# The low half of x in a gated linear attention with FFN: a GpSimd subtraction for nine units

## The chip, the cores and the metric

The kernel runs on one core of one Trainium2 chip. The metric is the device time of one execution in microseconds, median of several runs. The core has five engines that matter here: TensorE (PE, with its weight loads as PEld), VectorE (DVE), ScalarE (ACT), GpSimd (POOL) and the queue of SyncE (SPq) that issues the DMAs. Each works through its own list of instructions in order and waits on semaphores for the others.

## The reference

A gated linear attention runs over 4 batches, 8 heads, 768 steps and a head size of 48, all in float32; a feed-forward layer follows on the 3072 tokens:

```python
for t in range(S):
    state = alpha[:, :, t, :, None] * state + np.einsum('bhd,bhe->bhde', k[:, :, t], v[:, :, t])
    y[:, :, t] = np.einsum('bhd,bhde->bhe', q[:, :, t], state)
x = np.ascontiguousarray(y.transpose(0, 2, 1, 3)).reshape(B * S, H * D)
h = x @ w_in
g = np.maximum(0.01 * h, h)
out = (g @ w_out).astype(np.float32)
```

`x` is 3072 x 384, `w_in` 384 x 2048 and `w_out` 2048 x 384. The weights arrive as 64-bit floats.

## The kernel before

**Units and blocks.** The attention is cut into 24 units, each one chunk of 128 steps of one batch (`units`, six chunks by four batches). Three units make a block of 384 tokens, so the feed-forward layer has eight blocks, and it walks through the hidden dimension in 16 slices `f` of 128. The first nine units (`AHEAD`) are worked ahead of the bulk of the feed-forward layer, by `attention` (L518); the other fifteen are woven into it by `attention_later` (L548).

**One unit.** `scans` (L315) brings alpha into channel-by-time form, for the first nine units by four TensorE transposes into a PSUM bank (L287), and runs the running products (`pc`, four VectorE scans) and the reversed scan (`rc`). `scaled_q` and `scaled_k` multiply q and k by them (`qs`, `ks`). `scores` multiplies `ks` by `qs` on TensorE into two banks (16 matmuls, issued at L465). `mask_scores` (L377) copies them to SBUF on ScalarE (`sm`, L384) and zeroes the upper triangle on GpSimd (L385), one instruction for each of two halves; behind the masks GpSimd also runs the pending state scalings (L391). `k_tokens` transposes `ks` back (L398, evicted at L400), and `sum_up` (L344) makes a range check on ScalarE. `past`, `values` and `products` are the matmuls that make the unit's output y in one PSUM bank and the new state; `past` exists from each batch's second chunk on, that is from unit 4. `values` reads the masked scores. `split` (L469) then takes y out of PSUM.

**Low and high halves.** All feed-forward products are made from two halves: a value rounded to the fast matmul format (`fp32r`), called high, and the rest, called low. A slice of the first layer is nine matmuls, three 128-row groups by three pairs (high by high, high weight by low x, low weight by high x), at L597. ScalarE then makes 0.01 h (L602), VectorE the maximum (L605), ScalarE the high half of g (L607), VectorE its low half (L611), and nine matmuls at L626 make the second layer. In `split`, x's high half is a ScalarE copy from PSUM (L476), and its low half a VectorE subtraction, y from PSUM minus the high half from SBUF (L477). VectorE instructions of the attention are issued through the helper `vector` (L276), so the trace has them on that line: the subtraction is the one that writes `large`, the tile that holds x.

**Converting the weights.** `converting` (L248 to L268) turns a slice of 64-bit weights into a high and a low 32-bit half with two ScalarE instructions and six VectorE instructions; five of these read and write SBUF tiles alone. Slices 0, 1 and 2 are converted while units 6, 7 and 8 run; the others run beside the first two blocks of the feed-forward layer (`items` alternates blocks 0 and 1 over f, then takes blocks 2 to 7 one at a time).

**What sets the order.** Within the first nine units the order in each engine's list is not written out: the build puts each instruction where it becomes ready, earlier-traced ones first, on a timeline of its own. `tc.issue_after` (through `behind`) pins single ones: state scalings behind the mask, the first weight loads behind certain loads of v, the first conversions behind `AFTER` and `BEGIN`. One of these keys is `("xh", 6)`, the ScalarE copy of unit 6 in `split`. PSUM tiles of the attention come from two rings of three banks (`a` and `b`); a bank is free again when its last reader is done. `gather` (L507) moves the last rows of x into place by DMA after each third unit.

## Time and profile before

| What | Value |
| --- | --- |
| Median of 3 runs | 524.14 us (523.52 to 524.3) |
| The profiled execution's own time | 523.46 us |
| Its span in the profile | 521.7 us |
| TensorE busy | 507.4 us, 97% of the span |
| VectorE busy | 380.4 us, 73% |
| ScalarE busy | 236.0 us, 45% |
| GpSimd busy | 75.9 us, 15% |
| Granted TensorE clock, mean | 0.997 |
| The nine subtractions in VectorE's list, start | 17.56, 22.37, 27.18, 32.02, 37.79, 44.69, 51.80, 59.34, 65.81 us |

The span is the time from the first to the last instruction in the profile; 1.76 us of the execution's own time lie outside it. Shares are averages over stages with different limits: GpSimd's 15% over the whole span is 4 to 5 tenths in each slice of the first 65 us and nothing from there to 150 us. In the rows of the trace, a time in brackets at the end of a row is idle time of that engine just before the instruction, with what ended it. Matmuls overlap, so a matmul's duration (some 0.27 to 0.34 us) is longer than the step from one to the next.

### The profile page before, as it was taken

To read this page: it belongs to the slowest core of one execution; us is meant where nothing else is said; L and a number is where in the kernel's file an instruction comes from. 1 tells how busy PE (TensorE), PEld (TensorE's weight loads), DVE (VectorE), ACT (ScalarE), POOL (GpSimd) and SP (SyncE) were. 2 spreads that over 40 slices of the span, in tenths; PEclk is the share of its full clock that TensorE was granted. 3 is DMA by queue.
4 is the path that set the end of the run, shared out by engine and by line. 5 is a ranking of instruction groups with operands and counts; after the bars stand their busy time and mean duration, and the time that the engine had idled before them with its cause. 6 is when DMAs were issued, how large, how long until landed. Compare 5 with 4: busy or idle time off the path is not lost.

```text
span 521.7 us, 10758 instructions
## 1 busy us (share of the span) xinstructions
PE 507.4 (97%) x4178; PEld 487.6 (93%) x4178; DVE 380.4 (73%) x710; ACT 236.0 (45%) x504; POOL 75.9 (15%) x143
## 2 busy tenths in 40 slices
PE   8998999999999999999999999999999999999995
PEld 8787899999989889999999999999999999999995
DVE  6999999999999776778587677686586683333331
ACT  1765755555544543444443543453443542334331
POOL 4555500000001201121120120102102000000000
PEclk9999999999999999999999999999999999999998
DMA  9999985445715431542233421523421001001001
GB/s 145 163 186 187 233 178 134 121 123 143 178 32 151 118 72 44 123 97 85 63 76 65 128 69 32 122 57 89 99 57 40 27 21 25 0 1 45 1 0 52
DMA packets 92985, 46.68 MB, mean 89 GB/s; under 512 B 57856, under 2 KB 90112, under 8 KB 92928
## 3 DMA queue, kind: packets, MB, share of 16 engines
q1 hardware_dynamic: 92928, 45.93, 40.5%
q8 instruction: 35, 0.57, 0.5%
q14 instruction: 22, 0.18, 0.1%
HBM read 38.83 MB, written 4.72 MB: 83 GB/s over the span
## 4 chain that ended last, share of the span: by engine, by line
PE 72%; DVE 16%; DMA 5%; issue 3%; SPq 2%; ACT 1%; DVEq 0%; ACTq 0%
PE b L626 29%; PE ph L597 28%; PE a L465 8%; DMA raw<-in_moe_w_in_dram 3%; DVE pw L265 2%; DVE bits L254 2%; DVE bits L263 2%; PE b L465 2%; DVE gl L611 2%; DVE t L605 2%; PE ph L465 1%; DVE bits L251 1%; PE a L398 1%; PE b L287 1%; DVE pw L261 1%
## 5 line engine op out<-in xcount | busy, mean ns | idle before, releaser
L597 PE MATMUL ph<-large,w 128*128 128x384 f32 x1152 | 224.5, 336 | 1.1 <-DVE t L605 0.8
L597 PEld LDWEIGHTS ph<-large,w 128*128 128x128 f32 x1152 | 200.6, 188 | 3.4 <-DVE t L605 1.1
L626 PE MATMUL b<-w,gh 128*128 128x384 f32 x672 | 168.9, 338 | 0.6 <-DVE t L605 0.6
L605 DVE TENSOR_TENSOR t<-ph,t 128x384 f32<-128x384 f32 x128 | 70.6, 552 | 98.5 <-ACT t L602 98.1
L602 ACT ACTIVATE t<-ph 128x384 f32<-128x384 f32 x128 | 62.6, 489 | 136.0 <-PE ph L597 135.6
L626 PEld LDWEIGHTS b<-w,gh 128*128 128x128 f32 x672 | 119.6, 188 | 2.2 <-DVE t L605 0.8
L607 ACT CAST gh<-t 128x384 fp32r<-128x384 f32 x128 | 65.8, 514 | 95.2 <-DVE t L605 95.1
L626 PE MATMUL b<-w,gl 128*128 128x384 f32 x336 | 108.3, 335 | 0.0
L611 DVE TENSOR_TENSOR gl<-t,gh 128x384 fp32r<-128x384 f32 x128 | 70.7, 552 | 18.9 <-ACT gh L607 18.7
L626 PEld LDWEIGHTS b<-w,gl 128*128 128x128 f32 x336 | 62.7, 188 | 0.0
L385 POOL TENSOR_SCALAR_AFFINE_SELECT sm<-sm 128x512 f32<-128x512 f32 x33 | 24.7, 760 | 129.1 <-ACT sm L384 115.4
L335 POOL COPY small<-up 128x4 f32<-128x4 f32 x15 | 4.7, 313 | 199.6 <-DVE up L276 199.6
L465 PE MATMUL a<-qs,ks 48*64 48x128 f32 (+1 forms) x552 | 26.3, 272 | 3.0 <-DVE ks L276 1.5
L465 PEld LDWEIGHTS a<-qs,ks 48*64 48x64 f32 (+1 forms) x552 | 22.4, 140 | 4.7 <-ACT gh L607 1.5
L384 ACT COPY sm<-a 128x512 f32<-128x512 f32 x24 | 14.0, 583 | 14.7 <-PE b L465 12.5
L626 PE MATMUL a<-w,gh 128*128 128x384 f32 x96 | 20.5, 334 | 0.0
L276 DVE TENSOR_TENSOR_SCAN up<-e,small 128x128 f32<-128x128 f32 x60 | 20.4, 402 | 0.0
L276 DVE TENSOR_TENSOR_SCAN down<-e,small 128x511 f32<-128x511 f32 x15 | 19.2, 1282 | 0.7
L391 POOL TENSOR_TENSOR small<-small 48x192 f32<-48x192 f32 x32 | 19.0, 595 | 1.2
L257 ACT CAST w<-bits 128x768 fp32r<-128x768 f32 x16 | 13.4, 838 | 9.2 <-DVE bits L254 8.5
L276 DVE STREAM_TRANSPOSE e<-small 128x512 f32<-128x512 f32 x15 | 17.2, 1144 | 0.0
L626 PEld LDWEIGHTS a<-w,gh 128*128 128x128 f32 x96 | 17.0, 188 | 0.0
(106 smaller groups left out, 578.5 us busy)
## 6 DMA issues: line engine op xcount, KB each, us to landing
raw<-in_moe_w_out_dram SPq DMA_DIRECT2D x16, 384.0 KB, 4.0
small<-in_v_dram SPq DMA_DIRECT2D x24, 192.0 KB, 3.8
raw<-in_moe_w_in_dram SPq DMA_DIRECT2D x32, 144.0 KB, 4.4
out_dram<-o SPq DMA_DIRECT2D x24, 192.0 KB, 1.9
small<-in_alpha_dram SPq DMA_DIRECT2D x32, 96.0 KB, 2.2
small<-in_q_dram SPq DMA_DIRECT2D x30, 96.0 KB, 2.1
small<-in_k_dram SPq DMA_DIRECT2D x30, 96.0 KB, 2.2
small<-in_alpha_dram SPq DMA_DIRECT2D x30, 80.0 KB, 2.3
```

What stands on the lines that cost most here:

```text
L257: made["hi", f] = put(ordered, "ACT", lambda: nc.scalar.copy(hi, val))
L276: return put(u >= AHEAD, "DVE", lambda: op(*args))
L384: made["sm", u] = nc.scalar.copy(sm[s], ss[s])
L385: made["mask", u] = nc.gpsimd.affine_select(out=sm[s], in_=sm[s], compare_op=ALU.is_ge, fill=0.0, base=0, pattern=[[0, NP], [1, C]], chann ...
L391: nc.gpsimd.tensor_tensor(*scalings.pop(0))
L465: made["product",] = nc.tensor.matmul(out, weights, moving, start=start, stop=stop, skip_group_check=True)
L597: product = nc.tensor.matmul(ph, w_in_of(f, wn, g), xt[:, g, :], start=n == 0, stop=n == 3 * NG - 1)
L602: put(ordered, "ACT", lambda: nc.scalar.mul(t, ph, 0.01))
L605: put(ordered, "DVE", lambda: nc.vector.tensor_tensor(t, ph, t, ALU.max))
L607: put(ordered, "ACT", lambda: nc.scalar.copy(gh, t))
L611: made["gl", i, f] = put(ordered, "DVE", lambda: nc.vector.tensor_tensor(gl, t, gh.bitcast(F32), ALU.subtract))
L626: product = nc.tensor.matmul(po[j], gt[:, js], w_out_of(f, wn), start=f == 0 and n == 0, stop=f == NF - 1 and n == 2)
```

## The change

For the first nine units, `split` reads y from PSUM twice on ScalarE: one copy to a new SBUF tile `full` in full float32, one to the high half in `large` as before. The subtraction then runs on GpSimd, `full` minus the high half, both in SBUF. VectorE no longer takes part, and y's PSUM bank is now last read by the second ScalarE copy. `full` is 128 x 512 float32 with two buffers. The key `("xh", u)` now names the first of the two copies. Units 9 to 23 keep their form.

```diff
         xh, xl = (x_sb[0:BR, at:at + NP, n, j * C:(j + 1) * C] for n in (0, 1))
+        if u < AHEAD:
+            full = atp.tile([P, NP, C], F32, name="full")
+            made["xh", u] = nc.scalar.copy(full[0:BR], y[0:BR])
+            nc.scalar.copy(xh, y[0:BR])
+            made["x", u] = nc.gpsimd.tensor_tensor(xl, full[0:BR], xh.bitcast(F32), ALU.subtract)
+            return
         for h, l, t in [(xh, xl, y)] if u < AHEAD else [(xh[:, s::2, :], xl[:, s::2, :], pair[s]) for s in (1, 0)]:
             made["xh", u] = nc.scalar.copy(h, t[0:BR])
             made["x", u] = vector(u, nc.vector.tensor_tensor, l, t[0:BR], h.bitcast(F32), ALU.subtract)
```

## Prediction

> **What bounds the kernel now.** I read the page's head first, then the busy time of each engine by stage, cut at 28, 41 and 65 us, then the waits and the timelines within these stages.

> ```profile
> PE 507.4 (97%) x4178; PEld 487.6 (93%) x4178; DVE 380.4 (73%) x710; ACT 236.0 (45%) x504; POOL 75.9 (15%) x143
> 15.00:28.00 13.00, 12.55 (x167) 10.34 (x163) 12.67 (x28) 9.43 (x24) 7.30 (x18) 1.00 1.10 163
> 28.00:41.00 13.00, 12.83 (x181) 10.71 (x183) 11.38 (x25) 8.61 (x23) 7.62 (x17) 1.00 1.13 193
> 41.00:65.00 24.00, 21.66 (x274) 18.76 (x270) 23.48 (x43) 16.70 (x36) 13.78 (x16) 1.00 1.15 208
> 65.00:150.00 85.00, 84.58 (x485) 83.19 (x483) 84.94 (x136) 45.26 (x79) 0.00 (x0) 1.00 0.57 137
> ```

> Columns behind the length of the stretch: PE, PEld, DVE, ACT, POOL busy, each with its count, then the granted clock (1.00 throughout). TensorE carries the whole span. The nine subtractions lie in the first four stages, where VectorE is nearly full too: 97%, 88%, 98% and 100% of them. Two full engines can't both be the limit, so the question is what TensorE loses, and to whom. From 65 us on it loses next to nothing:

> ```profile
> 80.33 1.20 PE L626 MATMUL a<-w,gh 128*128 128x384 f32 x6
> 86.61 1.20 PE L626 MATMUL a<-w,gh 128*128 128x384 f32 x6
> 173.75 1.56 PE ph L597 x9
> 175.31 1.56 PE b L626 x9
> ```

> One weight slice for blocks 0 and 1 is 36 matmuls and takes 86.61 - 80.33 = 6.28 us. Later in the span, where nothing holds TensorE, nine take 1.56 us, so 36 take 6.24. VectorE sets the 6.28 here, but is worth only 0.04 us a slice: over the 85 us, some 13.5 slices, 0.5 us. Whatever VectorE is relieved of must therefore be turned into TensorE time before 65 us, and the rest is bounded by that 0.5.

> **What VectorE gives back, stage by stage.** The rows of its list around three of the subtractions (the ones that write `large`), and of TensorE where it stood waiting:

> ```profile
> 37.79 0.68 DVE L276 TENSOR_TENSOR large<-b,large 112x512 fp32r<-112x512 f32 x1
> 40.42 1.36 DVE L276 TENSOR_TENSOR_SCAN pc<-b,small 128x128 f32<-128x128 f32 x4 [0.75 <-PE b L287]
> 44.69 0.66 DVE L276 TENSOR_TENSOR large<-b,large 112x512 fp32r<-112x512 f32 x1
> 45.27 0.55 DVE L261 TENSOR_SCALAR pw<-bits 128x768 int32<-128x768 int32 x1
> 51.80 0.68 DVE L276 TENSOR_TENSOR large<-b,large 112x512 fp32r<-112x512 f32 x1
> ...
> 44.82 0.65 PE L287 MATMUL b<-small 128*128 128x128 f32 x4 [0.53 <-DVE rc L276]
> 49.54 0.37 PE L465 MATMUL a<-qs,ks 48*128 48x128 f32 x1 [0.60 <-DVE qs L276]
> 57.01 0.37 PE L465 MATMUL b<-qs,ks 48*128 48x128 f32 x1 [0.64 <-DVE qs L276]
> ...
> PEld ph L597 <- DVE w L268: 0.4, 1, 0.4
> ```

> A subtraction takes 0.66 to 0.68 us, but the next instruction starts 45.27 - 44.69 = 0.58 us after it, since they overlap; 0.58 is what leaves the list. Nine of them are 5.2 us. Most of that isn't on the path. Those before 40.42 us give nothing that lasts: VectorE then stands 0.75 us waiting for TensorE's transposes, and what it had saved would only lengthen that wait. From 40.42 to 150 us it never pauses for long, so the four subtractions of units 5 to 8 count, 4 x 0.58 = 2.3 us of VectorE.

> What of this reaches TensorE? The wait of 0.53 at 44.82 has no subtraction between it and the pause, so it stays. The 0.60 at 49.54 (scores waiting for `qs`) has one ahead of it, at 44.69: 0.58 comes back. The first feed-forward slice waits 0.4 for its low weights, behind the same one: 0.4 comes back. The 0.64 at 57.01 has a second ahead, at 51.80: 0.6 comes back. Sum 0.58 + 0.4 + 0.6 = 1.6 us. The subtractions of units 7 and 8 fall too late for a wait; they make VectorE's lead over the 6.28 us slices 1.2 us longer, which buys the 0.5 us above.

> A small third part: the bank of y is now free after two ScalarE copies, not after a ScalarE copy and a subtraction far down VectorE's list.

> ```profile
> PEld b L465 <- DVE large L276: 0.5, 3, 0.2
> 20.66 0.58 ACT L476 CAST large<-b 112x512 fp32r<-112x512 f32 x1 [0.35 <-PE b L465]
> 21.78 0.59 ACT L384 COPY sm<-a 128x512 f32<-128x512 f32 x1 [0.54 <-PE b L465]
> 22.27 0.60 ACT L384 COPY sm<-b 128x512 f32<-128x512 f32 x1
> ```

> Weight loads waited 0.5 us on it in all, in three places; they run beside matmuls, so I take 0.2 of it. Each unit's scores are then no later for ScalarE's sake: after the copy at 20.66 it idles 0.54 us, and a second copy occupies 22.27 - 21.78 = 0.49 us of it. That is the cover for the nine added copies (4.4 us of ScalarE in all); where it is gone, the `sm` copies behind slide by up to 0.5 us a unit. ScalarE is busy 70% of 41 to 65 us, so there I cost the copies at nothing.

> **What GpSimd takes on.** No GpSimd subtraction of this size is in the trace. The nearest rows, before and after 41 us:

> ```profile
> L385 POOL TENSOR_SCALAR_AFFINE_SELECT sm<-sm 128x512 f32<-128x512 f32 x10 | 6.1, 636 | 5.0 <-ACT sm L384 5.0
> L391 POOL TENSOR_TENSOR us<-us,small 112x192 f32<-112x192 f32 x4 | 2.0, 510 | 0.3
> L335 POOL COPY small<-pc 128x4 f32<-128x4 f32 x5 | 1.0, 190 | 4.9 <-DVE pc L276 4.9
> ...
> L385 POOL TENSOR_SCALAR_AFFINE_SELECT sm<-sm 128x512 f32<-128x512 f32 x6 | 6.3, 1064 | 5.3 <-ACT sm L384 5.3
> L391 POOL TENSOR_TENSOR small<-small 48x192 f32<-48x192 f32 x6 | 5.3, 875 | 0.2
> ```

> The mask, same size but one input, gives 0.64 us as a lower bound; the two-input product of 192 columns scaled whole by 512/192 gives 1.36 us as the upper. In between: 0.19 for an almost empty instruction plus (0.51 - 0.19)/188 a column, that is 0.19 + 508 x 0.0017 = 1.06 us. I take 1.06, because the two-input row is the same operation class. After 41 us GpSimd's instructions are 1.7 times as long (875 against 510), so 1.8 us there. [...]

> In total 5 x 1.06 + 4 x 1.8 = 12.5 us of GpSimd. It has room (7.30 of 13, 7.62 of 13, 13.78 of 24 used), but room in the mean is not room at the place: the next unit's mask is queued on the same engine, and TensorE waits for the mask.

> ```profile
> PEld b L465 <- POOL sm L385: 1.1, 3, 0.6
> ...
> 21.20 0.19 POOL L329 COPY rc<-small 128x1 f32<-128x1 f32 x1
> 22.44 1.22 POOL L385 TENSOR_SCALAR_AFFINE_SELECT sm<-sm 128x512 f32<-128x512 f32 x2 [1.06 <-ACT sm L384]
> 23.13 0.43 PE L465 MATMUL b<-sm,small 128*64 128x128 f32 x4
> 23.50 0.66 PE L287 MATMUL b<-small 128*128 128x128 f32 x4
> 32.09 1.22 POOL L385 TENSOR_SCALAR_AFFINE_SELECT sm<-sm 128x512 f32<-128x512 f32 x2 [1.05 <-ACT sm L384]
> 34.35 0.43 PE L465 MATMUL b<-sm,small 128*64 128x128 f32 x4
> ```

> The subtraction of unit 1 becomes ready when the second copy ends, 20.66 + 0.49 + 0.58 = 21.73. The mask of unit 2 becomes ready at 22.44. The subtraction is traced and ready first, so it goes first: it ends at about 22.8, and the mask starts 0.4 us late (0.7 at the upper price). The first `values` matmuls at 23.13 read the first half, done at 22.44 + 0.61 = 23.05: no slack. This holds for the masks of units 1, 2 and 3; from unit 4 on `past` stands between, and values follow the mask's start by 2.26 us (32.09 to 34.35), enough for the delay. So the price is 3 x 0.4 = 1.2 us, up to 3 x 0.7 = 2.1, unless TensorE has other work at that place. It has: the four transposes at 23.50 need no mask and take 0.66 us, their overlap with what follows included. The order is made by readiness; if it puts them ahead of `values`, they cover the 0.4 and the delay costs nothing. That is what I take.

> **Where VectorE and GpSimd meet.** In the third stage conversion instructions of VectorE that use SBUF alone run beside GpSimd, in the fourth they run alone:

> ```profile
> L263 DVE TENSOR_TENSOR bits<-bits,w 128x768 f32<-128x768 f32 x2 | 2.3, 1156 | 0.0
> L265 DVE SCALAR_TENSOR_TENSOR pw<-raw,pw 128x768 f32<-128x768 uint32 x2 | 2.2, 1098 | 0.0
> ...
> L263 DVE TENSOR_TENSOR bits<-bits,w 128x768 f32<-128x768 f32 x14 | 13.3, 948 | 0.0
> L265 DVE SCALAR_TENSOR_TENSOR pw<-raw,pw 128x768 f32<-128x768 uint32 x14 | 13.3, 952 | 0.0
> ```

> Each is 0.15 to 0.21 us longer beside GpSimd, and GpSimd's own instructions 1.7 times as long. At about 0.1 us of VectorE for each of the four late subtractions, I take 0.4. [...]

> **The sum**, on the profiled execution (523.46 us, of it 521.7 span; 0.68 below the median, and the differences carry over): waits 1.6, slices 0.5, banks 0.2, together 2.3 less; against it the contention, 0.4; masks covered, 0. That is 1.9 us less: 524.14 - 1.9 = 522.2 us.

> **Rivals.**
> - *Masks late.* As above, with `values` kept in front of the transposes: +1.2 to +2.1 on the 1.9 gained, so 523.4 to 524.3 us, centre 523.8. For it: the zero slack at 23.05. Against: the transposes at hand. Chance 0.33.
> - *GpSimd holds the conversions.* Each of the four late subtractions starts between two conversion instructions and stops VectorE for its 1.06 us or more. VectorE then loses 1.06 - 0.58 = 0.48 us a unit where it gained 0.58: 4 x 0.48 = 1.9 us more, 526.0 us. It decides as soon as a subtraction costs VectorE more than 0.58 us on average. Against it: the 0.21 us above is the most that a kind of instruction lost in the mean. [...] Chance 0.17.
> - *Nothing that lasts.* The next conversions start earlier only to wait for weights that arrive by DMA, as ScalarE's first step does already:

> ```profile
> ACT raw L248 <- DMA raw<-in_moe_w_in_dram: 2.1, 2, 1.3
> ```

> Those loads are queued behind a load of v that waits for TensorE, so they don't move until TensorE does. Of the 1.9 us then 0 to 0.7 are left, centre 523.8 us. Against it: VectorE, not ScalarE, is the full engine there. Chance 0.08.

> **Numbers.** The forecast has 0.42, with its own range 521.0 to 523.1: the upper end has the contention at 0.33 us a subtraction instead of 0.1, that is 0.9 more. About 0.2% (1.05 us) can be told from no change here. Faster by more: nearly all of the forecast and a little of the late masks, 0.43. Within: most of the late masks, and the last rival, 0.34. Slower: the held conversions, and late masks where ScalarE's copies slide too (another 3 x 0.5 us, 525.8 at most), 0.23. The range reaches from 521.0 (no contention, 0.4; the wait for `rc` of 0.53 recovered too; the whole 0.5 of the banks instead of 0.2) to 526.0 (the conversions held).

> **What would show it.** Right: VectorE's busy time falls by some 5 to 6 us; the waits at scores for `qs` after 41 us are gone, those of the transposes for `rc` are not; VectorE idles longer on transposes before 41 us; GpSimd shows nine subtractions of 1.06 us, 1.8 after 41 us; dense feed-forward work starts some 1.5 us earlier. Wrong: weight loads for `values` waiting for the mask by clearly more than the 1.1 us that they wait in 15 to 41 us now (late masks); L263 or L265 over 1.3 us in the mean beside the subtractions (held conversions); or a start of the dense stage that doesn't move.

## The result, and the profile after

| | before | after |
| --- | --- | --- |
| Median, 4 runs each | 524.22 us (523.52 to 524.30) | 527.43 us (526.04 to 527.99) |
| Ratio | | 1.0061, 95% interval 1.0045 to 1.0077 |
| The profiled execution and its span | 523.46, 521.7 us | 527.99, 526.3 us |

The kernel is 0.6% slower: +3.2 us where -1.9 us was forecast, and 1.4 us above the upper end of the range. In the changed kernel most line numbers rise by 6 or less: the first copy is L477, the second L478, the GpSimd subtraction L479; feed-forward matmuls are L603 and L632, the maximum t is L611. The conversion steps (L248 to L268), the masks (L385) and the attention matmuls (L465) keep theirs.

The head of the page of after:

```profile
PE 508.7 (97%) x4178; PEld 489.6 (93%) x4178; DVE 377.3 (72%) x701; ACT 240.3 (46%) x513; POOL 82.2 (16%) x152
```

Its busy time by stage (columns as in the prediction: PE, PEld, DVE, ACT, POOL, granted clock, DMA share, GB/s):

```profile
15.00:28.00 13.00, 11.69 (x159) 9.66 (x155) 10.71 (x24) 9.97 (x24) 9.43 (x19) 1.00 1.11 166
28.00:41.00 13.00, 12.08 (x162) 9.94 (x162) 9.98 (x22) 9.70 (x25) 10.58 (x19) 1.00 1.15 192
41.00:65.00 24.00, 20.47 (x273) 17.98 (x268) 20.99 (x38) 17.07 (x37) 17.12 (x22) 1.00 1.07 193
65.00:150.00 85.00, 85.00 (x506) 83.85 (x503) 84.80 (x135) 46.65 (x81) 1.30 (x1) 1.00 0.58 142
```

VectorE did lose its nine instructions. But in 15 to 65 us TensorE is busy 2.8 us less than before (12.55 + 12.83 + 21.66 against 11.69 + 12.08 + 20.47), and in 41 to 65 us VectorE, the full engine before (23.48 of 24), now idles 3.0 us. What VectorE was relieved of came out as idle time, and more than that.

Three places carry the loss. **First, the masks.** GpSimd and TensorE around unit 2 of after:

```profile
22.14 1.28 POOL L479 TENSOR_TENSOR large<-full,large 112x512 fp32r<-112x512 f32 x1 [0.41 <-ACT large L478]
23.36 1.23 POOL L385 TENSOR_SCALAR_AFFINE_SELECT sm<-sm 128x512 f32<-128x512 f32 x2
24.06 0.43 PE L465 MATMUL b<-sm,small 128*64 128x128 f32 x4 [0.68 <-POOL sm L385]
24.42 0.66 PE L287 MATMUL b<-small 128*128 128x128 f32 x4
```

The mask stood at 22.44 before; now the subtraction goes ahead of it and it starts at 23.36, 0.92 us late. The four transposes still come behind `values` (24.42 behind 24.06), so they cover nothing, and TensorE waits 0.68 us. The waits of after in 15 to 41 us (total, times, longest) put this together, three times:

```profile
PEld b L465 <- POOL sm L385: 2.7, 3, 0.9
PE b L465 <- POOL sm L385: 2.0, 3, 0.7
```

Before, weight loads waited 1.1 us there. The `values` of unit 4 start at 36.04 us, 1.69 later than the 34.35 of before.

**Second, VectorE's order.** The timelines of VectorE and TensorE in after, around units 7 and 8:

```profile
47.16 1.20 DVE L263 TENSOR_TENSOR bits<-bits,w 128x768 f32<-128x768 f32 x1
48.28 1.38 DVE L265 SCALAR_TENSOR_TENSOR pw<-raw,pw 128x768 f32<-128x768 uint32 x1
49.58 0.68 DVE L276 TENSOR_TENSOR qs<-b,pc 128x512 f32<-128x512 f32 x1
50.19 0.68 DVE L276 TENSOR_TENSOR ks<-a,rc 128x512 f32<-128x512 f32 x1
50.92 0.37 PE L465 MATMUL a<-qs,ks 48*128 48x128 f32 x1 [0.97 <-DVE ks L276]
...
57.84 0.94 DVE L265 SCALAR_TENSOR_TENSOR pw<-raw,pw 128x768 f32<-128x768 uint32 x1
58.71 0.68 DVE L276 TENSOR_TENSOR ks<-a,rc 128x512 f32<-128x512 f32 x1
59.31 0.54 DVE L611 TENSOR_TENSOR t<-ph,t 128x384 f32<-128x384 f32 x1
59.44 0.37 PE L465 MATMUL b<-qs,ks 48*128 48x128 f32 x1 [2.03 <-DVE ks L276]
```

In the kernel before, `ks` of unit 7 came ahead of both conversion steps, and `ks` of unit 8 and t ahead of the second pair. VectorE's timeline there:

```profile
55.21 0.68 DVE L276 TENSOR_TENSOR ks<-a,rc 128x512 f32<-128x512 f32 x1
...
56.28 0.68 DVE L276 TENSOR_TENSOR qs<-b,pc 128x512 f32<-128x512 f32 x1
56.88 0.54 DVE L605 TENSOR_TENSOR t<-ph,t 128x384 f32<-128x384 f32 x1
57.34 0.94 DVE L263 TENSOR_TENSOR bits<-bits,w 128x768 f32<-128x768 f32 x1
58.21 0.94 DVE L265 SCALAR_TENSOR_TENSOR pw<-raw,pw 128x768 f32<-128x768 uint32 x1
```

Now conversion steps have moved ahead. TensorE's two waits for `qs` (0.60 and 0.64) are gone, as forecast; waits of 0.97 and 2.03 for `ks` stand in their place. And VectorE itself stops, by the waits of after in 41 to 65 us:

```profile
DVE bits L251 <- ACT raw L248: 1.9, 1, 1.9
```

The first step of the next conversion is queued on ScalarE behind unit 8's copies, which are late too. The first whole nine-matmul feed-forward slice starts at 67.21 us, against 65.10 before.

**Third, the clock.** Much later TensorE waits once for ScalarE's output copy, 1.51 us where it had waited 0.95 for VectorE before, and right behind that its granted clock falls. TensorE's timeline of after, and three stretches of busy time by window (the granted clock is the third number from the end):

```profile
172.80 1.09 PE L465 MATMUL a<-qs,ks 48*64 48x128 f32 x28 [1.51 <-ACT o L646]
```

```profile
174.00:175.00 1.00, 1.00 (x5) 0.90 (x6) 0.90 (x2) 0.66 (x2) 0.00 (x0) 0.56 0.82 235
175.00:176.00 1.00, 1.00 (x6) 1.00 (x5) 0.38 (x1) 1.00 (x4) 0.00 (x0) 0.50 0.78 246
...
177.00:178.00 1.00, 1.00 (x6) 1.00 (x6) 0.00 (x0) 0.00 (x0) 0.76 (x2) 0.74 0.35 86
```

The clock record has half rate for 3.413 us there, from 174.1 to 177.5: some 1.7 us of work lost. The four executions of after agree: 526.04 us at a mean clock of 0.997, and 527.39 to 527.99 us at 0.993 to 0.995. So of the 4.6 us between the two profiles, about 1.7 are this stretch, and it isn't in every execution.

### The profile page after: what moved, and what is told of

The parts are those of the page before. It is cut to its first block, busy times and chain, and to the rows that moved or that the text cites. A ratio compares the mean times of both kernels' runs of the same rounds, so it can differ in the third digit from the quotient of the medians.

```text
span 526.3 us, 10766 instructions
## 1 busy us (share of the span) xinstructions
PE 508.7 (97%) x4178; PEld 489.6 (93%) x4178; DVE 377.3 (72%) x701; ACT 240.3 (46%) x513; POOL 82.2 (16%) x152
## 4 chain that ended last, share of the span: by engine, by line
PE 71%; DVE 17%; DMA 5%; issue 3%; SPq 1%; ACT 1%; POOL 1%; DVEq 0%; ACTq 0%
PE b L632 29%; PE ph L603 27%; PE a L465 7%; DMA raw<-in_moe_w_in_dram 3%; DVE pw L265 2%; DVE bits L254 2%; DVE bits L263 2%; PE b L465 2%; DVE gl L617 2%; PE ph L465 1%; DVE w L268 1%; DVE t L611 1%; DVE bits L251 1%; PE b L287 1%; DVE pw L261 1%
## 5 line engine op out<-in xcount | busy, mean ns | idle before, releaser
L603 PE MATMUL ph<-large,w 128*128 128x384 f32 x1152 | 224.4, 336 | 1.1 <-DVE t L611 0.8
L603 PEld LDWEIGHTS ph<-large,w 128*128 128x128 f32 x1152 | 200.8, 188 | 3.1 <-DVE t L611 1.4
L632 PE MATMUL b<-w,gh 128*128 128x384 f32 x672 | 169.9, 339 | 0.0
L611 DVE TENSOR_TENSOR t<-ph,t 128x384 f32<-128x384 f32 x128 | 70.7, 552 | 100.4 <-ACT t L608 99.9
L632 PEld LDWEIGHTS b<-w,gh 128*128 128x128 f32 x672 | 120.1, 189 | 1.5 <-issue 0.7
L632 PE MATMUL b<-w,gl 128*128 128x384 f32 x336 | 108.9, 336 | 0.0
L632 PEld LDWEIGHTS b<-w,gl 128*128 128x128 f32 x336 | 63.1, 189 | 0.0
L385 POOL TENSOR_SCALAR_AFFINE_SELECT sm<-sm 128x512 f32<-128x512 f32 x33 | 24.3, 750 | 123.6 <-ACT sm L384 115.0
L335 POOL COPY small<-up 128x4 f32<-128x4 f32 x15 | 4.8, 317 | 199.0 <-DVE up L276 199.0
L465 PE MATMUL a<-qs,ks 48*64 48x128 f32 (+1 forms) x552 | 26.7, 272 | 3.9 <-DVE ks L276 2.4
L465 PEld LDWEIGHTS a<-qs,ks 48*64 48x64 f32 (+1 forms) x552 | 22.5, 140 | 5.7 <-ACT o L646 1.7
L632 PE MATMUL a<-w,gh 128*128 128x384 f32 x96 | 20.5, 334 | 0.0
L276 DVE TENSOR_TENSOR_SCAN up<-e,small 128x128 f32<-128x128 f32 x60 | 20.4, 403 | 0.0
L276 DVE TENSOR_TENSOR_SCAN down<-e,small 128x511 f32<-128x511 f32 x15 | 19.2, 1283 | 0.8
L384 ACT COPY sm<-a 128x512 f32<-128x512 f32 x24 | 14.0, 584 | 10.5 <-PE b L465 9.8
L391 POOL TENSOR_TENSOR small<-small 48x192 f32<-48x192 f32 x32 | 18.5, 577 | 1.2
L276 DVE STREAM_TRANSPOSE e<-small 128x512 f32<-128x512 f32 x15 | 17.1, 1142 | 0.0
L632 PEld LDWEIGHTS a<-w,gh 128*128 128x128 f32 x96 | 17.0, 188 | 0.0
```

Of the source, the lines that this page charges most:

```text
L276: return put(u >= AHEAD, "DVE", lambda: op(*args))
L384: made["sm", u] = nc.scalar.copy(sm[s], ss[s])
L385: made["mask", u] = nc.gpsimd.affine_select(out=sm[s], in_=sm[s], compare_op=ALU.is_ge, fill=0.0, base=0, pattern=[[0, NP], [1, C]], chann ...
L391: nc.gpsimd.tensor_tensor(*scalings.pop(0))
L465: made["product",] = nc.tensor.matmul(out, weights, moving, start=start, stop=stop, skip_group_check=True)
L603: product = nc.tensor.matmul(ph, w_in_of(f, wn, g), xt[:, g, :], start=n == 0, stop=n == 3 * NG - 1)
```

## The experiments

Theory 1: the masks are late and nothing covers them. Theory 2: with the subtraction gone, VectorE's conversion steps move ahead of `ks` and t. Rivals: GpSimd's subtractions hold VectorE's instructions; or the time that VectorE gains doesn't last. Runs that share a control ran on one chip; the kernel before had 523.9 us (e1 to e4), 524.07 (e5 to e8) and 523.91 (e9 to e12).

**e1 and e4: the mask first, for all units.**

```diff
             while scalings:
                 nc.gpsimd.tensor_tensor(*scalings.pop(0))
+            subtract_lows()
...
-            made["x", u] = nc.gpsimd.tensor_tensor(xl, full[0:BR], xh.bitcast(F32), ALU.subtract)
+            lows.append((u, xl, full[0:BR], xh.bitcast(F32), ALU.subtract))
```

> All nine GpSimd subtractions stay, but each is put behind the next unit's mask (unit 8's is not). If late masks cost the first 41 us (theory 1), TensorE's waits for the mask there fall from 2.7 us to about 1.1, the last unit-4 values start near 34.4 us instead of 36.0, and the time falls by about 1.7 us, to 525.7. If the loss is GpSimd and VectorE meeting at SBUF (rival), nothing before 41 us counts and the time stays at 527.4.

e1 took 527.91 us, ratio 1.0078 (1.0064 to 1.0091). The first step came as expected: `values` of unit 4 at 34.32 us. Behind it nothing was won: the waits for `ks` are 1.0 and 2.6 us, and half rate follows the second of them and one of 1.58 us near 175 us (granted clock 0.86 in 53 to 65 us, 0.66 in 175 to 180 us). e4 adds a fix of the order to e1:

```diff
+            steps = converting(converted)
             with behind("ks", u):
-                convert(converted)
+                every_step(islice(steps, 5) if u + 1 < AHEAD else steps)
+            halves.append((u + 1, steps))
             converted += 1
+        if halves and ("ks", halves[0][0]) in made:
+            after, steps = halves.pop(0)
+            with behind("ks", after):
+                every_step(steps)
```

> As e1, and the last three VectorE steps of conversions 0 and 1 are queued behind the ks of the next unit (7 and 8), as they came by themselves in the kernel before. Theories 1 and 2 together: both waits for ks gone, dense work starts 1 to 1.5 us earlier than before, 522.5 to 523.5. Rival: no better than e1.

e4 took 526.33 us, 1.0045 (1.0032 to 1.0058). The waits for `ks` are gone, but the deferred gathers brought one of their own, 2.01 us of TensorE for x of block 0, whose gather was issued at 45.86 us (38.53 in the kernel before); half rate follows it (granted clock 0.86 in 53 to 65 us). That is a side effect of the edit; e1 and e4 decide theory 1 at its place and nothing more.

**e2 and e3: the change in two halves.**

```diff
-        if u < AHEAD:
+        if 0 <= u < 4:
             full = atp.tile([P, NP, C], F32, name="full")
```

> The new form for units 0 to 3 alone. Theory 1 (late masks): unit 4's values start near 36.0 us as in the changed kernel, and some 1.7 us stays until the end, 525.9; nothing of theory 2. Theory 2 (freed VectorE time lets conversion steps overtake ks) and the rival (GpSimd holds the conversions) have no place here: by them alone the time is that of before, 524.2.

> The new form for units 4 to 8 alone. The prediction's sum: 1.9 us less than before, 522.3. Theory 2: TensorE still waits for ks by 1 and 2 us in 41 to 65 us, 525 to 526. Rival (GpSimd holds the conversions): L263 and L265 above 1.3 us, 526. Theory 1 alone: no late masks, 524.2 or a little less.

e2 (units 0 to 3) took 525.13 us, 1.0022 (1.0013 to 1.0031); e3 (units 4 to 8, `4 <= u < 9`) 526.27 us, 1.0048 (1.0035 to 1.0061). The losses, 1.2 and 2.4 us, add up to a little more than that of the whole change. In e2 TensorE waits for the masks as in after, `values` of unit 4 start at 35.98 us, and the span is 1.6 us longer than before (523.3): the early delay isn't absorbed anywhere. In e3 unit 4 is on time (34.40) and TensorE waits 2.00 us for `ks` of unit 8. Both halves lose; the second was forecast to win.

**e5: the cover that the prediction counted on.** The transposes behind `values` of unit u are those of unit u+2, and their lines come later in the program. They are put ahead:

```diff
-                multiply([past(u), values(u), products(u)])
+                if u in (1, 2, 3):
+                    begun[u + 2] = scans(u + 2)
+                    next(begun[u + 2])
+                with behind("T", u + 2, 0) if u in (1, 2, 3) else nullcontext():
+                    multiply([past(u), values(u), products(u)])
```

> The changed split for units 0 to 3 only, as in e2_early_only, and besides the four transposes of the unit after next, which TensorE does behind the values of units 1, 2 and 3, are queued ahead of those values. This is the cover that the prediction counted on and that the changed kernel did not get. The prediction's cover step: the masks are still late by 0.4 to 0.7 us, but TensorE has 0.66 us of other work at that place; the waits of values for the mask fall to 0.2 us or less each, values of unit 4 start at about 34.3 us as before (35.98 in e2), and the time is that of the kernel before, 523.9 us. Rival, the delay is paid in any order: VectorE's next scans are the real path and the masks come late for it anyway; 525.1 us as in e2. A third outcome, transposes that are earlier by 0.7 us are worth something of their own to VectorE, which waits 3.3 us in four places for them: below 523.9 us.

e5 took 524.15 us against 524.07, ratio 0.9999 (0.9990 to 1.0007). TensorE's timeline of e5 at unit 2, and its waits in 15 to 41 us:

```profile
23.27 0.60 PE L287 MATMUL a<-small 128*128 128x128 f32 x4
23.80 0.43 PE L465 MATMUL a<-sm,small 128*64 128x128 f32 x4
```

```profile
PEld b L287 <- DVE rc L276: 2.1, 4, 0.7
...
PE b L287 <- DVE rc L276: 0.8, 3, 0.3
```

No wait for a mask is left above 0.2 us. The profile still has `values` of unit 4 at 34.98 us, 0.6 later than before, now through waits of the transposes themselves (0.8 us for `rc`, 0.5 for alpha's DMA); in the time nothing is left of it. Theory 1 is shown, with its size: 1.2 us, and gone with the order of four transposes at each of three units.

**e6: VectorE's order alone, no subtraction moved.** The kernel before, with `ks` of units 7 and 8 put behind L265 (`rest`) of the two early conversions:

```diff
-        put(ordered, "DVE", lambda: nc.vector.scalar_tensor_tensor(
+        made["rest", f] = put(ordered, "DVE", lambda: nc.vector.scalar_tensor_tensor(
...
-        made["ks", u] = vector(u, nc.vector.tensor_tensor, ks, kT, rc, ALU.mult)
+        with behind("rest", u - 7):
+            made["ks", u] = vector(u, nc.vector.tensor_tensor, ks, kT, rc, ALU.mult)
```

> The kernel before, with all subtractions on VectorE and nothing on GpSimd; only VectorE's order is changed: ks of unit 7 is queued behind the step L265 of the first early conversion, ks of unit 8 behind L265 of the second, which is the order that VectorE took by itself in the changed kernel. Theory of the order: TensorE's scores of units 7 and 8 wait for ks for about 1 and 2 us, the dense stage starts 1 to 2 us later than before, and the time is 525 to 526 us with no subtraction moved at all. Rival, contention of GpSimd and VectorE in SBUF or the fuller DMA queues made units 5 to 8 slow: nothing of that is here, 523.9 us, no difference.

e6 took 526.28 us, ratio 1.0047 (1.0029 to 1.0064); one of its seven executions, at 2824.16 us, isn't in the ratio. TensorE's waits in 49 to 62 us:

```profile
49.73 0.34 PE L466 MATMUL a<-qs,ks 48*128 48x128 f32 x1 [0.53 <-DVE ks L276]
59.51 0.37 PE L466 MATMUL b<-qs,ks 48*128 48x128 f32 x1 [3.04 <-DVE ks L276]
```

2.2 us are lost with not one subtraction moved to GpSimd. Part of it is the clock: half rate follows the wait of 3.04 us (granted clock 0.86 in 53 to 65 us). The one execution that shows no such stretch (mean clock 0.999) took 525.69 us, still 1.6 above the 524.07. So this order costs time by itself. The edit overstates it at unit 8 (3.04 against 2.03 in after) and understates it at unit 7.

**e7, e8 and e9: the order restored.** e7 is e3 with the edit of e4 (the last three VectorE steps of the first conversion behind `ks` of unit 7, those of the second behind `ks` of unit 8); e8 is all nine units, with e5's and e7's edits.

> The changed split for units 4 to 8 only, as in e3_late_only, and besides the last three VectorE steps of the first two early conversions are queued behind ks of units 7 and 8, as they came in the kernel before; the gathers are issued where the changed kernel issues them. Theory of the order: the waits for ks of 1 to 2 us are gone, the dense stage starts at 65.1 us or earlier and the time is at most 524 us; if the prediction's 1.6 us of recovered waits exist, about 522.3 us. Rival, the loss of e3 does not come from the order but from what the subtractions on GpSimd delay: 526 us as in e3.

> The changed kernel, all nine units, with both corrections: transposes ahead of the values of units 1 to 3 as in e5, and the last steps of the first two early conversions behind ks of units 7 and 8 as in e7. If both losses are as told (masks not covered, 1.6 us of span; ks behind conversions, 2 to 3 us), what is left is the prediction's own sum, 522 to 523 us; if they are not, it stays at 525 us or above. A fall below 523.9 us also means that the unit-9 scores near 170 us no longer find their bank taken by ScalarE's output copy, since that wait of 1.5 us and the half clock behind it came only in versions that reached that place late.

e7 took 527.34 us, 1.0069 (1.0056 to 1.0082), and e8 527.69 us, 1.0068 (1.0054 to 1.0081). Both miss what theory 2 expected (e8 still waits 1.79 us for `ks` of unit 8), and the timelines of VectorE and GpSimd in e7 show why, twice over:

```profile
57.31 0.94 DVE L265 SCALAR_TENSOR_TENSOR pw<-raw,pw 128x768 f32<-128x768 uint32 x1
57.80 1.59 POOL L479 TENSOR_TENSOR large<-full,large 112x512 fp32r<-112x512 f32 x1 [1.42 <-ACT large L478]
58.18 2.03 DVE L263 TENSOR_TENSOR bits<-bits,w 128x768 f32<-128x768 f32 x1
60.13 0.55 DVE L611 TENSOR_TENSOR t<-ph,t 128x384 f32<-128x384 f32 x1
```

t still came behind the conversion steps, 3.25 us later than in the kernel before (56.88), and with it `gh` and unit 8's copies on ScalarE. And L263, 0.94 us alone, took 2.03: it ended 0.82 us after the subtraction (57.80 + 1.59 = 59.39, 58.18 + 2.03 = 60.21), so it did nearly all its work when the subtraction was over. This is the held conversion of the prediction's rival, seen at one instruction. e9 restores the place of the conversion steps L263 to L268, the second time behind t (`qs` and L261 still go ahead of `ks`, as in after):

```diff
+            if converted < 2:
+                halves.append(((("ks", 7), ("t", 0, 0))[converted], steps))
```

> The changed split for units 4 to 8 only, as in e3_late_only, with VectorE's order of the kernel before restored at both places where it had changed: the last three steps of the first early conversion behind ks of unit 7 (as in e7), and those of the second behind the maximum t of the first feed-forward slice, which in the kernel before came ahead of them (in e7 it came 3 us later, and with it ScalarE's copies of unit 8 and the next conversion). Theory of the order: t is done at about 57 us, ScalarE's copies of unit 8 start at about 58.5 us, the dense stage starts at 65.1 us or earlier, and the time is at most 524 us; with the prediction's recovered waits 522.3 us. Rival, GpSimd's subtractions hold the conversion steps beside which they run (L263 took 2.03 us once in e7 beside one): about 1 us of VectorE is lost there in whatever order, and the time stays at 525 us or more.

e9 took 525.61 us, ratio 1.0037 (1.0025 to 1.0049): 1.7 us above its control where e7 was 3.3 above its own, still slower than before. t is done by 58.4 us, and the wait for `ks` of unit 8 is 0.52 us. But a subtraction met another conversion step, in the same two timelines of e9:

```profile
60.11 1.69 POOL L479 TENSOR_TENSOR large<-full,large 112x512 fp32r<-112x512 f32 x1 [3.14 <-ACT large L478]
60.84 1.78 DVE L268 TENSOR_TENSOR w<-pw,bits 128x768 fp32r<-128x768 f32 x1
```

L268 takes 0.94 us in the kernel before; here it ends 0.82 us after the subtraction.

**e10 and e11: no subtraction at all.** e3 and e9 with the low half of x of units 4 to 8 not computed; zeros written at the start stand in its place.

```diff
-            made["x", u] = nc.gpsimd.tensor_tensor(xl, full[0:BR], xh.bitcast(F32), ALU.subtract)
```

> As e3_late_only, but the low part of x of units 4 to 8 is not computed at all: the two ScalarE copies stay, the GpSimd subtraction is left out (the low part is zeros written at the start). VectorE's order is that of e3. Theory of the order: the kernel is slower than the kernel before by 1 to 2 us although less work is done, since TensorE waits for ks behind conversion steps as in e3 (about 2 us at unit 8): 525 to 526 us. Rival, GpSimd's own instructions (their contention with VectorE, the mask behind them) make units 4 to 8 slow: without them nothing is lost and VectorE's 2.9 us are gained, 522.5 us or less.

> As e9_late_order, but with the GpSimd subtraction of units 4 to 8 left out as in e10 (low part zeros). The difference to e9 is the price of the GpSimd subtractions in the restored order, the difference to e10 that of VectorE's order without any subtraction. If the prediction's step holds that VectorE's freed time recovers 1.6 us of waits in the old order, this one takes 522 to 522.5 us; if the freed time only lengthens other waits (weights by DMA, v), 523.9 us. Contention would show as e9 slower than this by 1 us or more.

| late units, units 0 to 3 as before | subtraction on GpSimd | no subtraction |
| --- | --- | --- |
| VectorE's order as it came | e3: 526.27 us, 1.0048 (1.0035 to 1.0061) | e10: 525.15 us, 1.0021 (1.0008 to 1.0033) |
| The conversion steps put back (e9) | e9: 525.61 us, 1.0037 (1.0025 to 1.0049) | e11: 523.66 us, 0.9996 (0.9985 to 1.0006) |

This square sets the two causes side by side. By its medians, down the right column the order costs 1.5 us and down the left 0.7, where the two intervals overlap; along the lower row the GpSimd subtractions cost 1.95, along the upper 1.1. e10 does less work than the kernel before and has the slower median: it waits for `ks` much as e3 does (2.00 us at unit 8 there), with no subtraction to blame. TensorE's waits of e10, in 48 to 60 us and near 172 us:

```profile
49.76 0.37 PE L468 MATMUL a<-qs,ks 48*128 48x128 f32 x1 [0.65 <-DVE ks L279]
58.29 0.37 PE L468 MATMUL b<-qs,ks 48*128 48x128 f32 x1 [2.03 <-DVE ks L279]
171.90 1.18 PE L468 MATMUL a<-qs,ks 48*64 48x128 f32 x28 [1.53 <-ACT o L648]
```

But the clock is in these medians. Half rate follows the second and the third of these waits, and one such stretch takes 0.003 off the mean clock. e10's six executions at a mean clock of 0.998 or more have a median of 524.15 us, the other six 525.69. At 0.998 or more the kernel before has 523.92 here, e9 525.05 and e11 523.30. Among such executions the order costs 0.85 us (e10 against e11), the subtractions 1.75 (e9 against e11), and e10 is within 0.25 us of the kernel before. e3 has no such execution (0.991 to 0.996), and half rate in its profile follows the wait of 1.53 us near 172 us (granted clock 0.82 in 170 to 175 us). So much of what the order costs in the upper row comes through half rate; what e3, or the whole change, would lose without it, no run shows.

And e11, with all 2.9 us of VectorE's five late subtractions gone, the conversion steps in their place and nothing in exchange on GpSimd, gains 0.25 us, inside the interval of no change; the second ScalarE copies are in it, so they cost nothing that shows. Its waits, 41 to 66 us:

```profile
DVE bits L254 <- DMA raw<-in_moe_w_in_dram: 1.6, 1, 1.6
PE b L468 <- DMA small<-in_v_dram: 0.9, 1, 0.9
```

VectorE's gained time ends as a wait for the next weights (L254 is L251 of before), and TensorE waits for v. Of the 1.95 us between e9 and e11 the two profiles show 0.8 us between the `values` of unit 4 and the last matmul. Another 0.7 lies ahead of unit 4, where no subtraction has been moved, and 0.6 behind the last matmul; so how much of the 1.95 is the subtractions' stays open.

**e12: everything together**, all nine units, e5's and e9's edits.

> The changed kernel for all nine units, with the transposes of the unit after next ahead of the values of units 1 to 3 (e5) and VectorE's order of the kernel before restored at both places (e9). Units 0 to 3 are then neutral (524.15 us in e5 against 524.07). By the theory of the order the rest behaves as e9: 522 to 524 us. If the subtractions on GpSimd themselves cost VectorE time, 525 us or more.

e12 took 525.22 us, ratio 1.0028 (1.0014 to 1.0041): with the masks covered and the conversion steps put back, 1.3 us of the 3.2 are left. That is of the size of e9's loss (1.7), which goes with the subtractions on GpSimd; a wait of 1.25 us for `ks` of unit 8 is left too. No version with the change beats the kernel before, and e11 bounds what the late units could win: with the work left out there are 0.25 us to be had, 0.8 by the end of the interval.

## Why the prediction was wrong

- **Right:** the subtractions before 40.42 us give nothing that lasts. With the masks covered, units 0 to 3 end where they began (e5). The two waits for `qs` after 41 us went, the one of 0.53 for `rc` stayed, and nine subtractions left VectorE's list.
- **"They cover the 0.4 and the delay costs nothing" failed.** The delay was told, and its price (1.2 to 2.1 us) held 1.69 in the profile; the cover was hoped for. The transposes belong to a unit two further on, and nothing put them first. e5 shows the step was right about what a cover would do, and wrong that there was one. Its price carried through: 1.2 us (e2).
- **"Sum 0.58 + 0.4 + 0.6 = 1.6 us" failed.** Each term assumed VectorE's list with one entry struck out. The list came out in another order, with waits for `ks` of 0.97 and 2.03 us instead of those for `qs`. e6 shows that such an order loses time with no subtraction moved; how much of the change's 3.2 us is the order's alone stays open, since half rate and the held steps come with it. Even in the old order the sum wouldn't have come: e11 gives 0.25 us. That is the third rival, "nothing that lasts" (chance 0.08), by the loads that it named and those of v. That the conversions were what came last there was read from VectorE's busy share, and not from when its inputs land.
- **The GpSimd subtraction** was sized at 1.06 us, later 1.8; it took 1.28 and 1.44. The first lies inside the bounds of 0.64 to 1.36, the second below the 1.8. The groups of GpSimd in after, up to 41 us and from there to 70 us:

```profile
L479 POOL TENSOR_TENSOR large<-full,large 112x512 fp32r<-112x512 f32 x5 | 6.4, 1278 | 1.7 <-ACT large L478 1.6
L479 POOL TENSOR_TENSOR large<-full,large 112x512 fp32r<-112x512 f32 x4 | 5.7, 1436 | 4.7 <-ACT large L478 4.7
```

- **Contention, taken as 0.4 us, was mis-sized, and its sign in the rival was right.** The test that was set (L263 or L265 above 1.3 us in the mean) came out against the rival: 1.08 and 1.16 us in after. That test was too narrow: in after the one that is held is L261, in the dense stage, 1.36 us instead of 0.55. The timelines of GpSimd and VectorE there:

```profile
67.02 1.30 POOL L479 TENSOR_TENSOR large<-full,large 112x512 fp32r<-112x512 f32 x1 [2.55 <-ACT large L478]
67.37 1.36 DVE L261 TENSOR_SCALAR pw<-bits 128x768 int32<-128x768 int32 x1
```

  0.8 us of VectorE at a place where it is full, in after; 1.3 in e9 (L268, and L261 at 66.91 with 1.05), 1.9 in e7. Where it strikes depends on what stands beside each subtraction. In after `ks` and a scan, which read PSUM, passed beside a subtraction without delay (`ks` at 58.71 beside the one at 58.52: 0.68 us; `pc` at 51.65 beside the one at 51.10: 1.36 us; both as ever). That a late subtraction stops VectorE for its whole length was the rival's assumption, which no row of the kernel before shows.
- **Slices (+0.5)** didn't come: VectorE is busy 84.80 of the 85 us from 65 on, as before, and TensorE, 2.1 us late at 67.21, is 2.55 late at its next long wait (over at 152.95 us, 150.40 before).
- **Not foreseen:** the bank of the scores near 170 us, and the clock behind it (some 1.7 us in most executions of after). The long wait there, 1.51 to 1.58 us for ScalarE's output copy, stands in the profiles of after, e1, e3 and e10 and in no other; these are the versions with two copies in the late units and conversion steps ahead of `ks`. So it seems to come with the order; why is not traced.
- **VectorE's busy time** fell by 3.1 us, not 5 to 6. The held L261 is 0.8 of the difference; the rest wasn't traced to single places.

## What to carry to other kernels

Striking an instruction out of an engine's list gives a new list: ask what else will be ready at that moment and go ahead, and price that order, before any gain is summed up from the old one. A cover counts only if something makes it run first; find the line that orders it. When VectorE is relieved by GpSimd, look at each place where the two will meet in SBUF (L263 took 2.03 us instead of 0.94 at one of them in e7), not at the mean, and ask of the freed time what input it would wait for next; leaving the work out altogether (e11) bounds the gain for the price of one run. Where half rate can follow a long wait, as it did behind 1.51 us in after, look at the clock of each execution before setting one median against another.

## What the runs showed of the hardware

Conversion steps of VectorE, in SBUF alone, that started during a GpSimd subtraction did most of their work after that had ended: L263 2.03 us instead of 0.94 in e7, L268 1.78 instead of 0.94 in e9, L261 1.36 instead of 0.55 in after. Working in SBUF alone isn't what decides it: a RECIPROCAL with one input of 32 columns in SBUF took its usual 0.31 us at 51.89 in e7, beside the subtraction at 51.67. Where VectorE's stood first, the GpSimd one was longer (1.77 us at 51.10 in after, begun while L268 ran, against 1.28). What the two engines share there, no run shows. The prediction, looking at the means of the kernel before, had not taken such holds as the likeliest case.

```profile
53.00:65.00 12.00, 9.97 (x109) 8.71 (x108) 9.93 (x16) 8.71 (x20) 5.65 (x8) 0.86 1.08 226
53.00:65.00 12.00, 10.00 (x138) 8.86 (x137) 9.94 (x15) 9.41 (x23) 7.86 (x9) 1.00 1.05 223
```

The clock records show what goes with it. In the profiles of before and after, every stretch of full rate that half rate ends is a whole number of 3.413 us (in after 167.253 is 49 of them and 344.746 is 101), so one can count steps of 3.413 us from the first record. Of the 2.03 us of e10, 1.57 fall into one step. The 2.00 of e3 are split by a step's end into 0.75 and 1.26, and the 2.03 of after at 59.44 us into 0.65 and 1.38; neither is followed by half rate. In the profiles of before and after, up to the last matmul, half rate follows the one step in which TensorE idled for 1.51 us, and none in which it idled for 1.38 or less. Of the waits in the other twelve from 30 us on, half rate follows those of 1.53 to 3.04 us (in e1, e3, e4, e6, e8 and e10), apart from the 2.00 of e3, and none of 1.30 or less. The 1.51 us are less than half of a step.
